# Recurrent chunks of the third and fourth batch at every second slot instead of every third, in a fused mLSTM, Fourier and MLP kernel

## The chip, the cores and the metric

The kernel runs on one core of one Trainium2 chip. Its time is the device time of one execution in microseconds; 439.55 us is the median of three runs of the kernel before (439.53 to 440.16). Five engines each work through an instruction list of their own and wait for one another by semaphores: PE multiplies matrices, DVE (VectorE), ACT (ScalarE) and POOL (GpSimd) do elementwise work, and SP issues the DMAs.

## What is computed

Two blocks, one after the other, on four batches of 768 tokens. The first is a recurrence over time for eight heads of 40 features; its output is the input `x` (768 x 320) of the second. The second adds to `x` the real part of a two-dimensional Fourier transform, normalizes, and adds a two-layer MLP (320 to 1280 to 320):

```python
for t in range(S):                                   # _attn_ref
    m_new = np.maximum(f_gate[:, :, t] + m, i_gate[:, :, t])
    f_stab = np.exp(f_gate[:, :, t] + m - m_new)
    i_stab = np.exp(i_gate[:, :, t] - m_new)
    C = f_stab * C + i_stab * outer(vt, kt)
    n = f_stab * n + i_stab * kt
    denom = np.maximum(np.abs(n @ qt), 1.0)
    y[:, :, t] = sigmoid(o_gate[:, :, t]) * (C @ qt) / denom
...
X = np.fft.fft(np.fft.fft(x, axis=1), axis=2)        # _moe_ref
u = x + np.real(X)
un = (u - mu) / np.sqrt(var + 1e-06)
out = u + np.maximum(un @ w_ch1, 0.0) @ w_ch2
```

## The kernel before

**Tiling.** Each batch is cut into six chunks of 128 tokens (`NT = 6`). Batches are numbered 0 to 3 here, so the change concerns batches 2 and 3. For each chunk the recurrence becomes a handful of matrix products: scores of queries and keys (`mlstm_scores`, L456, into two PSUM tiles `ps`), the contribution of the state carried in (`mlstm_from_state`, L470, into `ph`), that of the chunk itself (`mlstm_from_chunk`, L477, into the same `ph`), and the update of the state (`mlstm_to_state`, L487, into `pc`). Around them: ACT takes exponentials of a decay matrix `W` (`mlstm_exp`, L412, four heads at a time), POOL masks it (`mlstm_mask`, L434), scales the queries (L422) and the values (L428) and decays the state (L446), DVE multiplies the scores into `W` (`mlstm_weigh`, L462), `mlstm_gather` adds `pc` to the state on DVE (L504, L506) and copies `ph` to `hT` on ACT (L508 to L519), `mlstm_turn` transposes `hT` on PE into `px` (L526), and `mlstm_finish` divides and gates on DVE (L535 to L541) and leaves a slice of `x`.

**The Fourier mix** of a batch follows its six chunks: `mix_fold` (DVE, L595 to L607) adds and subtracts pairs of chunks, three folds a batch; then products `pz`, `pzt` (L635 to L638) and `pu` (L669), `mix_add` (DVE, L684 to L694, six a batch), `mix_center` (ACT, L702), transposes `put` (L709) and copies `uT` (ACT, L714).

**The MLP** of batches 1 to 3 has two stages. In the first, five blocks of four steps (`mlp_block`, L829 and L834) form the first layer from sums of its inputs; its four PSUM banks are freed by ACT copies and by DVE additions (L838), and POOL applies the ReLU (L841). In the second, twelve half products per batch (`mlp_out`, L882) form the second layer in PSUM tile `po`, and after every second one `mlp_store` (DVE, L888) writes a tile of the output. `mlp_sums` (DVE, L817) prepares the sums of the first stage just before it begins.

**Order.** The program is laid out by hand. A call `at(slot, phase, fn, ...)` puts work into a numbered slot, and `run` emits slots in order, within a slot by phase (`EVAC` 0, `FILL` 1, `MAIN` 2, `FILL_PE` 3) and at equal phase in the order of the `at` calls, which go batch by batch. Every engine executes its own instructions in the order in which they were emitted. `MAIN` holds one MLP step or half product per slot. The MLP of batch 1 takes slots 63 to 82 for its first stage and 83 to 94 for its second; batch 2 takes 95 to 114 and 115 to 126. Slots 51 to 62 hold the second products of batch 0.

Chunk `c` of a batch starts at slot `s = s0 + stride * c`: exponentials at `s` and `s + 1`, scores at `s`, mask at `s + 1`, `mlstm_weigh` and the state's decay at `s + 2`, the products with state and chunk and the state's update at `s + 3`, `mlstm_gather` at `s + 4`, transposes at `s + 5` to `s + 8`, and `mlstm_finish` a slot later. With stride 3, batch 2 (from slot 50) and batch 3 (from slot 82) have their last two chunks partly beside the first stage of another batch's MLP.

**Buffers.** `ps` has two PSUM banks, so the scores of one chunk wait until the chunk before it has been weighed; `ph`, `pc` and `px` share two banks; the MLP and the mix share four. In SBUF the queries and keys and `W` have three buffers each, `Gb` and `qg` two each, keys and values four.

Of the kernel before, what the change touches and what calls it, by code (L numbers as in the profile page):

```python
# [20 lines left out]
NT = S // L  # L21
# [29 lines left out]
def kernel(  # L51
# [61 lines left out]
    def at(slot, phase, fn, *args):  # L113
        plan.setdefault((slot, phase), []).append((fn, args))
# [7 lines left out]
    EVAC, FILL, MAIN, FILL_PE = range(4)  # L122
# [421 lines left out]
    def plan_mlstm(b, s0, stride=3):  # L544
        for c in range(NT):
            s = s0 + stride * c
            if b > 0:
                t = 22 + 2 * c if b == 1 and c < 3 else s - 5
                at(t, FILL, mlstm_load, b, c)
                at(t, FILL, mlstm_load_max, b, c)  # L550
                at(t, FILL, mlstm_load_decay, b, c)
                at(s, FILL, mlstm_load_o, b, c)
            if (b, c) > (0, 0):
                at(s, FILL, mlstm_exp, b, c, 0)
                at(s + 1, FILL - 0.5, mlstm_exp, b, c, NP)
                last = (b, c) == (0, NT - 1)
                at(s - 1 if last else s, FILL_PE + (2.05 if last else 2), mlstm_scores, b, c)
                if b > 0:
                    at(s + 1, FILL, mlstm_mask, b, c)
            at(s, FILL, mlstm_scale_v, b, c)  # L560
            at(s if (b, c) == (0, 2) else s + 1, FILL + 0.1, mlstm_scale_q, b, c)
            at(s + 2, FILL, mlstm_decay, b, c)
            end = (b, c) == (0, NT - 1)
            at(s + 1 if end else s + 2, FILL - 0.4 if end else FILL, mlstm_weigh, b, c)
            at(s + 2 if end else s + 3, FILL_PE, mlstm_from_state, b, c)
            at(s + 2 if end else s + 3, FILL_PE + (2 if end else 3), mlstm_from_chunk, b, c)
            at(s + 3, FILL_PE + 3, mlstm_to_state, b, c)
            at(s + 3 if end else s + 4, FILL, mlstm_gather, b, c)
            if b == 0:
                t, x = ((8, 11), (11, 14), (13, 14), (14, 15.5), (17, 18), (18, 21))[c]  # L570
            else:
                t = s + (8, 8, 7, 5, 5, 5)[c]
                x = t + 1
            at(t, FILL_PE + ((2.5 if c < 4 else 1) if b == 0 else 1), mlstm_turn, b, c, b == 0 and c < 4)
            at(x, FILL + 0.05, mlstm_finish, b, c)
# [157 lines left out]
    def plan_mix(b, s0, x_done, s_feat, s_add, s_turn):  # L733
        for j in range(TG):
            p = TG - 1 - j
            at(x_done[j], FILL + 0.5, mix_fold, b, p)
            if b == 0:
                at((s0 - 4, s0 - 2, s0)[j], FILL_PE + 4, mix_seq, b, p, (0, 1))
                at((s0 - 2, s0 - 2, s0)[j], FILL_PE + 4, mix_tail, b, p)
            else:  # L740
                at(s0, FILL_PE + 4, mix_seq, b, p, (0,))
                at(s0 + 1, FILL_PE + 4, mix_seq, b, p, (1,))
                at(s0 + 2, FILL_PE + 4, mix_tail, b, p)
        for i in range(2):
            at(s0 + 1 if b == 0 else s0 + 1 + i, FILL, mix_seq_out, b, i)
        at(s0 + (1 if b == 0 else 3), FILL + 0.1, mix_tail_out, b)
        for p in range(TG):
            at(s_feat[p], FILL_PE + 4, mix_feat, b, p)
        for c, a, t in zip(ORDER, s_add, s_turn):
            at(a, FILL, mix_add, b, c)  # L750
            at(t, FILL + 0.1, mix_center, b, c)
            at(t, FILL_PE + 5, mix_turn, b, c)
            if b > 0:
                at(t, FILL_PE + 6, mix_turn_out, b, c)
            elif t < s_mlp:
                at(t + 1, FILL + 0.2, mix_turn_out, b, c)
            else:
                at(t + 1, EVAC, mix_turn_out, b, c)
# [133 lines left out]
    MLP_SLOTS = NT // TG * (NFF + 2 * TG)  # L892

    def plan_mlp(b, s):
        groups = range(NT // TG)
        for i in range(NFF // 2) if b > 0 else ():
            for step in range(4):
                at(s, MAIN, mlp_block, b, i, step)
                s += 1
        for gr in groups if b == 0 else ():  # L900
            for f in range(NFF):
                at(s, MAIN, mlp_in, b, gr, f)
                s += 1
                if f % 2:
                    at(s, EVAC, mlp_relu, b, gr, f - 1)
                    at(s, EVAC, mlp_relu, b, gr, f)
        for gr in groups:
            for i in range(TG):
                for half in range(2):
                    at(s, MAIN, mlp_out, b, gr, i, half)  # L910
                    s += 1
                at(s, EVAC, mlp_store, b, gr, i)
# [3 lines left out]
    gates(gates_pool.enter_context(tc.tile_pool(name="gates", bufs=1)))  # L916


    def plan_batch(b, s_mlstm, s_mix, s_mlp):
        plan_mlstm(b, s_mlstm)  # L920
        done = [s_mlstm + 3 * (j + NT // 2) + 7 for j in range(NT // 2)]
        assert s_mix >= done[-1] and s_mlp >= s_mix + 9
        late = [s_mlp + 2 * c for c in range(TG)]
        if b == 0:
            feat = [s_mix + 1, s_mix + 1, s_mlp + 3]
            turn = [s_mix + 2, s_mix + 3, s_mix + 4]
            add = turn + [s_mlp, s_mlp + 4, s_mlp + 6]
            late = [s_mlp + 2, s_mlp + 5, s_mlp + 7]
        else:
            feat = [s_mix + 3, s_mix + 4, s_mix + 6]  # L930
            add = [s_mix + c for c in (4, 4, 5, 6, 7, 7)]
            turn = [s_mix + c for c in (5, 6, 6)]
            late = [s_mix + c for c in (7, 8, 8)]
            at(s_mlp - 1, FILL_PE + 7, mlp_sums)
        plan_mix(b, s_mix, done, feat, add, turn + late)
        at(s_mlp + NFF, FILL + 0.6, mix_rstd, b)
        plan_mlp(b, s_mlp)

    s_mlp = 31
    plan_batch(0, 0, 22, s_mlp)  # L940
    plan_batch(1, 32, 54, s_mlp + MLP_SLOTS)
    plan_batch(2, 50, 83, s_mlp + 2 * MLP_SLOTS)
    plan_batch(3, 82, 115, s_mlp + 3 * MLP_SLOTS)
    for n in range(4):
        at(s_mlp + 2 * NFF + 1 + n, FILL + 0.4, weight_sums, n)

# [130 lines left out]
```

## Time and profile before

| quantity | value |
|---|---|
| median of three runs | 439.55 us |
| the profiled execution | 440.03 us |
| its span, first to last instruction | 438.3 us |
| granted TensorE clock | 1.00 |
| second products of batch 0, slots 51 to 62 | 123.3 to 181.8 us |
| first stage of batch 1's MLP, slots 63 to 82 | 181.8 to 225.9 us |
| scores of batch 3's chunk 0 at the end of slot 82, then second products of batch 1, slots 83 to 94 | 225.9 to 285.0 us |
| first stage of batch 2's MLP, slots 95 to 114 | 285.0 to 325.9 us |

What a slot is worth differs: the ten matmul instructions of one half product of the second layer take 2.69 us by the chain of waits, one block of four slots of the first stage 6.4 us (205.70 to 212.1 us in the timeline of PE). The profile prints a matmul with its end modelled, so neighbouring rows overlap by some tenths; the distance from one start to the next is the better measure. About 1.7 us of the profiled execution lie outside its span.

### The profile page before, as it was taken

Reading aid. Unit: us, or ns where it says so; the run is one execution under the profiler, and the core shown is the slowest. Engines: PE = TensorE matmul, PEld = TensorE weight load, DVE = VectorE, ACT = ScalarE, POOL = GpSimd, SP = SyncE. Lnnn points to the kernel's source line nnn. Section 1 sums busy time; section 2 is a strip of 40 time slices with the busy share of each in tenths; the row PEclk is TensorE's granted clock in tenths of the full one; section 3 lists DMA queues with packets and bytes.
Section 4 is the critical chain, followed back from the end, with each engine's and each line's share of the span. In section 5 each row is a group of like instructions: output and inputs, shape, how many; then the busy total and the mean of one; then the engine's idle time right before and its main releaser. Section 6 shows DMA issues by size and latency. Waiting matters only on the chain.

```text
span 438.3 us, 7352 instructions
## 1 busy us (share of the span) xinstructions
PE 423.6 (97%) x2696; PEld 285.8 (65%) x2696; DVE 249.7 (57%) x617; ACT 169.6 (39%) x448; POOL 161.3 (37%) x180
## 2 busy tenths in 40 slices
PE   8998999999999999979999999999999999999997
PEld 6877555666577777656456778766456766445774
DVE  7799877589977176587622546677631552343111
ACT  6986376667544204543242334353220131232000
POOL 5554211365424303256581330536670000577000
PEclk9999999999999999999999999999999999999999
DMA  7799396669545424086003334200000000000000
GB/s 237 249 251 336 94 272 226 204 197 271 148 124 163 133 82 133 0 238 184 0 0 92 102 124 137 80 31 3 0 0 16 15 30 31 0 0 2 30 30 30
DMA packets 20547, 47.11 MB, mean 107 GB/s; under 512 B 2784, under 2 KB 9312, under 8 KB 20384
## 3 DMA queue, kind: packets, MB, share of 16 engines
q1 hardware_dynamic: 20512, 46.65, 34.8%
q8 instruction: 21, 0.34, 0.4%
q14 instruction: 14, 0.11, 0.1%
HBM read 42.52 MB, written 4.11 MB: 106 GB/s over the span
## 4 chain that ended last, share of the span: by engine, by line
PE 78%; DVE 12%; issue 4%; DMA 2%; ACT 2%; POOL 1%; SPq 0%; ACTq 0%; POOLq 0%; DVEq 0%
PE po L882 30%; PE pm L829 13%; PE ps L456 5%; PE ph L477 5%; PE ph L470 4%; PE pu L669 4%; PE pm L834 3%; PE pz L638 3%; PE pm L770 3%; PE px L526 2%; PE put L709 2%; PE pzt L638 2%; DMA raw<-in_w 1%; DVE W L462 1%; PE pc L487 1%
## 5 line engine op out<-in xcount | busy, mean ns | idle before, releaser
L882 PE MATMUL po<-w_sb,hT 128*128 128x320 f32 x480 | 135.2, 434 | 0.0
L882 PEld LDWEIGHTS po<-w_sb,hT 128*128 128x128 f32 x480 | 89.7, 190 | 38.1 <-issue 2.0
L841 POOL TENSOR_SCALAR hT<-hT 128x384 f32<-128x384 f32 x45 | 66.4, 1500 | 76.1 <-DVE hT L838 75.8
L888 DVE SCALAR_TENSOR_TENSOR ot<-po,rstd,u 128x320 f32<-128x320 f32 x24 | 13.2, 548 | 69.9 <-PE po L882 69.9
L838 DVE TENSOR_TENSOR hT<-hT,pm 128x384 f32<-128x384 f32 x60 | 30.5, 550 | 39.2 <-ACT hT L859 25.7
L434 POOL TENSOR_SCALAR_AFFINE_SELECT W<-W 128x1024 f32<-128x1024 f32 x18 | 21.0, 1169 | 86.3 <-ACT W L412 65.0
L412 ACT ACTIVATE W<-W,colT 128x128 f32<-128x128 f32 x144 | 45.1, 396 | 0.0
L829 PE MATMUL pm<-uT,w_sb 128*128 128x384 f32 x90 | 32.8, 493 | 2.5 <-DVE hT L838 2.4
L462 DVE TENSOR_TENSOR W<-ps,W 128x512 f32<-128x512 f32 x48 | 30.6, 679 | 6.9 <-POOL W L434 6.7
L770 PE MATMUL pm<-uT,w_sb 128*128 128x384 f32 x80 | 29.8, 500 | 0.5 <-DVE u L691 0.4
L714 ACT COPY uT<-put 128x384 f32<-128x384 f32 x24 | 10.9, 479 | 48.0 <-PE put L709 48.0
L456 PE MATMUL ps<-qk 40*128 40x128 f32 x384 | 28.1, 284 | 0.0
L456 PEld LDWEIGHTS ps<-qk 40*128 40x128 f32 x384 | 23.7, 187 | 4.5 <-issue 1.0
L477 PE MATMUL ph<-W,kvt 128*41 128x128 f32 x384 | 25.8, 277 | 0.0
L422 POOL TENSOR_TENSOR qg<-qk,Gb 128x512 f32<-128x512 f32 x18 | 25.5, 1414 | 0.1
L470 PEld LDWEIGHTS ph<-qg,C 128*128 128x128 f32 x160 | 20.2, 191 | 7.8 <-issue 4.2
L829 PEld LDWEIGHTS pm<-uT,w_sb 128*128 128x128 f32 x90 | 16.0, 190 | 14.0 <-DVE hT L838 6.4
L470 PE MATMUL ph<-qg,C 128*128 128x128 f32 x160 | 21.7, 279 | 2.6 <-DVE x L541 1.0
L834 PE MATMUL pm<-uT,w1t_sb 64*128 64x384 f32 x120 | 23.9, 509 | 0.0
L477 PEld LDWEIGHTS ph<-W,kvt 128*41 128x41 f32 x384 | 19.5, 117 | 3.0 <-DVE fe L602 0.2
L515 ACT COPY h<-ph 41x512 f32<-41x512 f32 (+1 forms) x16 | 9.3, 580 | 28.8 <-PE ph L477 28.7
L702 ACT ACTIVATE uc<-u 128x384 f32<-128x384 f32 x24 | 14.1, 612 | 15.0 <-DVE u L694 15.0
(166 smaller groups left out, 641.3 us busy)
## 6 DMA issues: line engine op xcount, KB each, us to landing
W<-M_d SPq DMA_DIRECT2D x18, 512.0 KB
kvt<-in_kv SPq DMA_DIRECT2D x24, 324.0 KB
qk<-in_qkT SPq DMA_DIRECT2D x48, 160.0 KB
raw<-in_w SPq DMA_DIRECT2D x10, 640.0 KB
Gb<-G_d SPq DMA_DIRECT2D x36, 128.0 KB
so<-in_o SPq DMA_DIRECT2D x24, 160.0 KB
out<-ot SPq DMA_DIRECT2D x24, 160.0 KB
ds_sb<-in_dft_s SPq DMA_DIRECT2D x1, 1155.0 KB
```

The lines of the kernel that those rows point to most:

```text
L412: nc.scalar.activation(out=k.W[:, h, :], in_=M, func=AF.Exp, scale=-1.0, bias=colT[:, c, 0, b * H + h:b * H + h + 1])
L422: nc.gpsimd.tensor_tensor(out=k.qg, in0=k.qk[:, 0], in1=k.Gb, op=OP.mult)
L456: nc.tensor.matmul(k.ps[hip][:, p, :], k.qk[r, 1, p, :], k.qk[r, 0, p, :], start=True, stop=True)
L462: nc.vector.tensor_tensor(out=Wv, in0=k.ps[hip], in1=Wv, op=OP.mult)
L470: nc.tensor.matmul(k.ph[:, p, :], k.C[:, p, :], k.qg[:, p, :], start=(p == 0), stop=False, skip_group_check=True)
L477: nc.tensor.matmul(k.ph[hip * 64:hip * 64 + D1, p, :], k.v1[:, 2 * p + hip, :], k.W[:, 2 * p + hip, :], start=(c == 0 and p == 0), stop=Tr ...
L770: nc.tensor.matmul(k.pm[i], w1_sb[:, ch, f0:f0 + L], u[2 * ch], start=(ch == 0), stop=False)
L829: nc.tensor.matmul(bank, w, u, start=start, stop=True, skip_group_check=True)
L834: nc.tensor.matmul(bank, block(w1t_sb, i)[rows], mlp_u(gr, 1)[rows], start=False, stop=True, skip_group_check=True)
L838: nc.vector.tensor_tensor(out=h, in0=h, in1=bank, op=OP.add)
L841: nc.gpsimd.tensor_scalar(out=h, in0=h, scalar1=-1.0, scalar2=0.0, op0=OP.mult, op1=OP.max)
L882: nc.tensor.matmul(k.po, k.h[gr][f][:, i * L:(i + 1) * L], w2_sb[:, f, :], start=(f == 0), stop=(f == NFF - 1))
```

## The change

The chunks of batches 2 and 3 come every second slot instead of every third, and start one slot later (51 and 83 instead of 50 and 82), so that all scores lie beside the second products of the batch before. Loads are issued later relative to the chunk, each kind at a slot of its own, and `mlstm_turn` is at `s + 6` for chunks 0 to 4 and `s + 5` for chunk 5. The folds follow the finished pairs of chunks, so they move too: for batch 2 from slots 66, 69 and 72 to 64, 66 and 68, for batch 3 from 98, 101 and 104 to 96, 98 and 100. Batches 0 and 1 and all of the mix and the MLP stay in their slots.

```diff
@@ plan_mlstm
             s = s0 + stride * c
             if b > 0:
-                t = 22 + 2 * c if b == 1 and c < 3 else s - 5
-                at(t, FILL, mlstm_load, b, c)
-                at(t, FILL, mlstm_load_max, b, c)
-                at(t, FILL, mlstm_load_decay, b, c)
-                at(s, FILL, mlstm_load_o, b, c)
+                t = [22 + 2 * c] * 3 if b == 1 and c < 3 else [s - 5] * 3 if stride > 2 else (s - 4, s - 2, s - 3)
+                at(t[0], FILL, mlstm_load, b, c)
+                at(t[1], FILL, mlstm_load_max, b, c)
+                at(t[2], FILL + 0.2, mlstm_load_decay, b, c)
+                at(s, FILL + 0.3, mlstm_load_o, b, c)
...
-                t = s + (8, 8, 7, 5, 5, 5)[c]
+                t = s + ((8, 8, 7, 5, 5, 5) if stride > 2 else (6, 6, 6, 6, 6, 5))[c]
                 x = t + 1
@@ plan_batch
-    def plan_batch(b, s_mlstm, s_mix, s_mlp):
-        plan_mlstm(b, s_mlstm)
-        done = [s_mlstm + 3 * (j + NT // 2) + 7 for j in range(NT // 2)]
+    def plan_batch(b, s_mlstm, s_mix, s_mlp, stride=3):
+        plan_mlstm(b, s_mlstm, stride)
+        done = [s_mlstm + stride * (j + NT // 2) + 7 for j in range(NT // 2)]
...
-    plan_batch(2, 50, 83, s_mlp + 2 * MLP_SLOTS)
-    plan_batch(3, 82, 115, s_mlp + 3 * MLP_SLOTS)
+    plan_batch(2, 51, 83, s_mlp + 2 * MLP_SLOTS, 2)
+    plan_batch(3, 83, 115, s_mlp + 3 * MLP_SLOTS, 2)
```

## The prediction, made before the changed kernel ran

> **What bounds the kernel now.** I read the page's busy times first, then the busy times of four stretches (the stages in which the moved work lies), then who waited for whom in them, and last the timelines of PE and DVE. The page says that PE is the bound:
>
> ```profile
> span 438.3 us, 7352 instructions
> PE 423.6 (97%) x2696; PEld 285.8 (65%) x2696; DVE 249.7 (57%) x617; ACT 169.6 (39%) x448; POOL 161.3 (37%) x180
> ```
>
> The four stretches, in order: second products of batch 0, first stage of batch 1, second products of batch 1 (with the scores of batch 3's chunk 0 ahead of them), first stage of batch 2.
>
> ```profile
> core 0: us, PE busy (x) PEld busy (x) DVE busy (x) ACT busy (x) POOL busy (x), PEclk, DMA share, GB/s
> 123.30:181.80 58.50, 58.50 (x416) 44.11 (x417) 32.14 (x84) 18.82 (x53) 14.47 (x19) 1.00 0.37 114
> 181.80:225.90 44.10, 40.33 (x210) 22.91 (x208) 30.74 (x81) 17.35 (x45) 26.97 (x23) 1.00 0.37 105
> 225.90:285.00 59.10, 59.10 (x429) 44.63 (x429) 26.64 (x74) 21.41 (x61) 20.10 (x24) 1.00 0.31 99
> 285.00:325.90 40.90, 39.72 (x209) 23.50 (x208) 26.61 (x76) 14.30 (x35) 23.07 (x20) 1.00 0.03 9
> ```
>
> Beside the second products PE is never idle. Beside the first stages it is idle for 44.10 - 40.33 = 3.8 and 40.90 - 39.72 = 1.2 us. The change moves PE work from the second and fourth stretch into the first and third and takes none away, so at most these 5.0 us can be won. Who PE waits for in 184.9 to 226.9 us:
>
> ```profile
> PE pm L829 <- DVE hT L838: 1.2, 2, 0.8
> PE ph L470 <- DVE x L541: 1.0, 1, 1.0
> PE px L526 <- DVE C L506: 0.6, 1, 0.6
> ```
>
> All of it is DVE coming late, which at this point is working off a queue (timeline of DVE): `mlp_sums` from 182.57, then a store, the gather, the weighing, two finishes, an addition, and a fold.
>
> ```profile
> 185.59 0.54 DVE L888 SCALAR_TENSOR_TENSOR ot<-po,rstd,u 128x320 f32<-128x320 f32 x1
> 186.05 0.67 DVE L506 TENSOR_TENSOR C<-C,pc 40x164 f32<-40x164 f32 x2
> 186.75 1.29 DVE L462 TENSOR_TENSOR W<-ps,W 128x512 f32<-128x512 f32 x2
> 189.11 0.49 DVE L541 TENSOR_TENSOR x<-px,so 128x320 f32<-128x320 f32 x1
> 189.52 0.54 DVE L838 TENSOR_TENSOR hT<-hT,pm 128x384 f32<-128x384 f32 x1
> 194.11 0.49 DVE L595 TENSOR_TENSOR eo<-x 128x320 f32<-128x320 f32 x1
> 195.46 0.32 DVE L602 TENSOR_TENSOR fe<-eo 128x159 f32<-128x159 f32 x1
> ```
>
> From starts to starts: sums 0.59 each, store 0.46, gather 0.70, weighing 1.21, finish 1.56 (187.96 to 189.52), fold 1.71 (194.11 to 195.82), addition 0.47.
>
> [...] the weighing at 174.71 (below) starts only when two whole `mix_add` are done. [...] `so<-so,den` (L539) took 1.36 us at 190.61, while POOL masked and scaled queries, and 0.49 at 188.58.
>
> **The change part by part.** PE prices, from starts in the timeline: scores of a chunk 1.09, from state 0.98, from chunk 1.00, state update 0.41, transposes 0.44.
>
> *Moved PE work.* Into each of the two stages of second products come two sets of scores, one chunk's three products and one set of transposes: 2.18 + 2.39 + 0.44 = +5.0. Out of each first stage go one set of scores, the same three products and one set of transposes: -3.9. The other set of scores leaves slot 50 or slot 82: -1.09. Sum zero.
>
> *Weighing just ahead of the next scores.* This decides. With stride 3, the scores of chunk c+1 came one slot after the weighing of chunk c, whose `ps` banks they need. With stride 2 both are in the same slot: PE reaches the scores after one half product (2.69), and by then DVE must have done all that it has in this slot ahead of the weighing. Where batch b's `mix_add`s are in the slot, they are emitted first (lower batch number), and they wait for `pu`, the last PE product of the slot before. The trace shows such a run of DVE work:
>
> ```profile
> 170.47 0.44 PE L669 MATMUL pu<-dd_sb,Zt 128*1 128x161 f32 x2
> 171.55 2.86 PE L882 MATMUL po<-w_sb,hT 128*128 128x320 f32 x10
> ...
> 170.95 0.33 DVE L684 TENSOR_TENSOR u<-x,pu 128x161 f32<-128x161 f32 x1 [1.17 <-PE pu L669]
> 174.61 0.18 DVE L694 BATCH_NORM_AGGREGATE u<-stats 128x2 f32<-128x6 f32 x1
> 174.71 1.26 DVE L462 TENSOR_TENSOR W<-ps,W 128x512 f32<-128x512 f32 x2
> ```
>
> Two `mix_add` take 3.3 us (155.86 to 159.17), with the row of their own as here 3.8. Slot by slot, from its first PE instruction:
> - slot 87 (batch 3): two adds 3.3, gather 0.7, weighing 1.3 = 5.3; PE is there at 2.7. Stall 2.6.
> - slot 61 (batch 2): adds begin 0.8 early (six transposes `put` stand between) and end at 3.0, gather 3.7, weighing 5.0; PE, with transposes of chunk 2 on the way, is there at 3.1. Stall 1.8.
> - slot 59: one add 1.7, gather and weighing to 3.7, PE at 3.1. Stall 0.6. Slot 89: its add needs no new `pu`, DVE is done at 1.7. None. Slots 53, 55, 57, 85, 91, 93 have no add ahead of the weighing (the two of slot 90 are over by then): DVE is done 0.5 to 2.5 after the slot's start. None.
> - slot 58: the state update of chunk 2 has been given the PSUM bank of its own `ph`, so it waits for the copies of `ph` on ACT (0.58 + 0.17 and two handovers). Stall 0.8. Slot 90: it waits for the finish of chunk 0 behind two adds, which ends as PE arrives. 0.1.
>
> Sum: 3.2 in the first stage of second products, 2.7 in the other. What queues behind the waiting scores on PE is everything: the rest of the slot and all later ones, and PE has no spare time to make it up.
>
> *First stages.* DVE loses a weighing, a gather and a finish here, but the folds come closer together and two of them ahead of the additions that free PE's banks. Batch 1's stage, from slot 63 at 0: DVE begins with the sums at 0.8 (as before: 182.57), is done with them at 3.1, store 3.6, gather 4.3, weighing 5.5, finish 7.1, fold 8.8, addition 9.2, finish 10.8, fold 12.5, three additions 13.9, finish 15.5, fold 17.2, addition 17.7. PE: transposes of chunk 3 until 2.0; from state waits for the gather (4.3 against 3.4); from chunk waits for the weighing (5.5 against 5.3); the tails of block 0 wait for the addition (9.2 against 8.5); block 1 waits for the next additions (13.0 against 11.6) and its own tails again (17.7 against 17.2). PE finishes block 1 at 19.6, and three more blocks of 6.4 with the 0.36 of idling that PE has at 212.83 behind the norm factors (L722 to L731) make 39.1; 0.2 for joints: 39.3 against 44.1. Batch 2's stage: `mlp_sums` are out of the way before it starts (its mix is three slots earlier), DVE runs ahead until the second fold: finish 3.6, fold 5.2, addition 5.7, finish 8.4, fold 10.1, additions from 10.5 (PE there at 9.4), last fold 14.7, addition 15.1 (PE 14.6). It ends at 36.9 against 40.9.
>
> So the first stages get shorter by 4.8 and 4.0, of which 3.9 each is the moved work: 1.0 us of idling is won, not 5.0, because the same DVE queue stands there with its folds pushed together.
>
> *Loads, masks, exponentials.* ACT needs about 2.6 for eight exponentials (8 x 0.32 by starts, 182.42 and 186.59) and some 1.2 for copies and the gate per chunk, POOL 1.17 + 1.41 + 0.82 + 2 x 0.50 = 4.4; a chunk now has two slots of 9 to 12 us. Both fit, and masks end a slot or more before the weighing. The loads of `W` are freed by the products at `s - 3` and asked for at `s - 2`: two slots for 512 KB, hidden unless a transfer takes over some 9 us. Their SP instructions stand behind an output store that waits for DVE, which in these slots is done early. I take 0; if the cover is gone, ACT, mask, weighing and scores slip, up to 3.
>
> *Joints.* Scores stand alone now; the half product after lone scores at 226.91 took 0.1 longer. Twelve places: 0 to 1.2, and as much may be saved where scores leave other products. I take 0.
>
> **Sum,** against the profiled execution: second products +5.0 + 3.2 and +5.0 + 2.7; slots 50 and 82 -1.1 each; first stages -4.8 and -4.0. Together +4.9, so 440.03 becomes 444.9. The median shown is 0.48 below that execution: 444.5.
>
> **Rivals.**
> 1. *Waits as reckoned* (chance 0.60): 444.5, its own range 442.0 to 447.5 (stalls of 59, 58 and 87 half or one and a half times their size, joints).
> 2. *The folds' move frees the first stages* (0.10, faster). One mechanism: additions that free PE's banks stop being late there, all 5.0 us of idling go, and the stalls in the second products come out under 3 us: 439.55 - 5.0 + 2.5 = 437. For it: DVE has 3.6 us less to do per first stage. Against: fold and finish stand ahead of the additions in the emitted order, as now. It decides in favour of faster as soon as the new stalls are below the idling that is won.
> 3. *An even trade* (0.08): stalls of 5.9 shrink to 1 or the idling won grows to match: 439.5.
> 4. *More than reckoned* (0.22): POOL, now busier beside the second products, holds up DVE's finishes and folds (0.9 each, as at 190.61; about four on the path), or loads of `W` land late (3): 444.5 + 4 = 448.5.
>
> **How the numbers follow.** About 0.2% is what a measurement here can tell from no change. Slower: rivals 1 and 4 and a little of 3, 0.84; within 0.2%: 0.06; faster 0.10. The range 439.5 to 449.5 leaves about 0.13 below and 0.06 above.
>
> **What would show it.** In the changed profile the scores (L456) of slots 61 and 87 wait for DVE's W (L462), 1.8 and 2.6 us; PE is idle some 6 us in the two stages of second products, where it is never idle now; the first stages last about 39 and 37 us with 1 to 1.4 us waits for hT (L838) at block 1. I am wrong if L456 has no waits, or if the first stages lose more than 6 us each.

## The result and the profile after

| | before | after |
|---|---|---|
| median | 439.56 us (439.19 to 440.94, 6 runs) | 452.82 us (451.84 to 455.75, 6 runs) |
| the profiled execution | 440.03 us | 452.77 us |
| its span | 438.3 us | 451.1 us |
| granted TensorE clock, mean of an execution | 1.00 in the profiled one | 0.989 to 0.996 in all six |

The ratio is 1.0304 with an interval of 1.0273 to 1.0335. The change makes the kernel 13.3 us slower: the direction forecast, more than twice the size (444.5), and above the range (up to 449.5).

The page of the kernel after, against the same lines of before:

```profile
span 451.1 us, 7344 instructions
PE 433.7 (96%) x2696; PEld 288.2 (64%) x2696; DVE 245.5 (54%) x617; ACT 169.0 (37%) x448; POOL 159.5 (35%) x180
PEclk9999999999999999999999979999999999999999
```

PE executes the same 2696 products and is busy 10.1 us longer with them (433.7 against 423.6). At an equal count the rows themselves have become longer. Part of that is waiting inside a row, which the profile counts as busy: the scores of slot 59 take 1.75 us (at 167.64) and no idling is shown ahead of them, where 1.16 is usual. Part is the clock: the one 7 in its row (slices of 11.3 us) shows where it fell.

The busy times of the four stages of after, each from the first product of the stage to the first of the next. The columns are the stretch, its length, the busy time of PE, PEld, DVE, ACT and POOL with counts, the granted clock, and the DMA share and rate:

```profile
core 0: us, PE busy (x) PEld busy (x) DVE busy (x) ACT busy (x) POOL busy (x), PEclk, DMA share, GB/s
121.37:189.68 68.31, 66.03 (x494) 49.11 (x493) 33.52 (x95) 25.36 (x75) 19.71 (x25) 1.00 0.32 96
189.68:229.53 39.85, 38.38 (x149) 19.80 (x148) 25.65 (x72) 11.69 (x27) 19.76 (x16) 1.00 0.37 98
229.53:300.58 71.05, 68.19 (x489) 50.62 (x487) 30.67 (x83) 25.73 (x75) 24.54 (x29) 0.95 0.32 93
300.58:338.45 37.87, 37.00 (x151) 19.65 (x148) 23.13 (x67) 10.97 (x25) 19.76 (x16) 1.00 0.01 4
```

I call them A (second products of batch 0), B (first stage of batch 1), C (second products of batch 1) and D (first stage of batch 2), and cut every kernel in this way. In the kernel before, the scores in slot 82 then belong to B.

| | start of A | A | B | C | D | D's end to the end of the span |
|---|---|---|---|---|---|---|
| before | 123.22 | 58.58 | 45.11 | 58.04 | 40.77 | 112.6 |
| after | 121.37 | 68.31 | 39.85 | 71.05 | 37.87 | 112.6 |
| difference | -1.85 | +9.73 | -5.26 | +13.01 | -2.90 | 0 |

A and C grow by 22.7 us, of which 10.0 is the work that moved into them; the rest of that growth, 12.7, is about as much as the whole profiled execution lost. Who PE waited for, over the whole span of after (engine, what, line, releaser: sum, times, longest):

```profile
PE ps L456 <- issue: 2.1, 1, 2.1
PE ps L456 <- DVE W L462: 1.3, 1, 1.3
...
PE pm L834 <- DVE hT L838: 0.9, 2, 0.5
...
PE pc L487 <- ACT h L519: 0.8, 1, 0.8
...
PE pc L487 <- DVE x L541: 0.6, 1, 0.6
```

The scores (L456) now wait twice as idling of PE, in slots 87 and 61, and the state's update (L487) in slots 58 and 90. The place of the longest of them, slot 87, in the timeline of PE of after (start, duration, what, and the idle time ahead of it):

```profile
251.45 2.85 PE L882 MATMUL po<-w_sb,hT 128*128 128x320 f32 x10
256.44 2.47 PE L456 MATMUL ps<-qk 40*128 40x128 f32 x16 [2.14 <-issue]
258.84 1.43 PE L669 MATMUL pu<-dd_sb,Z 128*128 128x161 f32 x4
260.07 1.27 PE L669 MATMUL pu<-dd_sb,Zt 128*128 128x320 f32 x2
261.13 4.30 PE L882 MATMUL po<-w_sb,hT 128*128 128x320 f32 x10
```

and DVE over the same time, of which the first row is the start of two `mix_add`, the second and third the end of them and the gather, the last the weighing:

```profile
251.65 0.33 DVE L684 TENSOR_TENSOR u<-x,pu 128x161 f32<-128x161 f32 x1 [2.04 <-PE pu L669]
...
254.87 0.18 DVE L694 BATCH_NORM_AGGREGATE u<-stats 128x2 f32<-128x6 f32 x1
254.97 0.65 DVE L504 COPY C<-pc 40x164 f32<-40x164 f32 x2
255.65 1.29 DVE L462 TENSOR_TENSOR W<-ps,W 128x512 f32<-128x512 f32 x2
```

Two additions take 3.32 us (251.65 to 254.97), gather and weighing 1.97; the scores start at 256.44, when the second of the weighing's two instructions is under way. DVE ran them in the order of emission: it stood idle for 2.04 us ahead of the first addition, waiting for `pu`, although the scores that this weighing takes had started at 242.87 (1.16 us) and the mask on POOL at 238.54 (1.09 us). The trace names "issue" for this wait, where it names DVE's `W` in slot 61: the releaser is inferred, and here the instruction that ends the wait is read from DVE's timeline. The wait is the one that the prediction gave for slot 87.

What it did not give is in the last row of PE. Ten products of a half take 4.14 us from their start to the next (261.13 to 265.27; 2.69 before), and the six products of `pu` 2.29 from their start to that of the half product (258.84 to 261.13), where those of slot 86 took 1.19 (250.26 to 251.45). The clock over this stretch of after, cut where it changes (columns as above, the clock third from the end):

```profile
253.81:257.22 3.41, 1.13 (x6) 0.51 (x6) 3.00 (x9) 0.82 (x3) 1.67 (x4) 1.00 0.74 223
257.22:260.64 3.42, 3.42 (x20) 3.00 (x20) 0.00 (x0) 0.00 (x0) 2.27 (x2) 0.50 0.00 0
260.64:264.05 3.41, 3.41 (x8) 2.23 (x7) 1.69 (x6) 0.00 (x0) 0.00 (x0) 0.50 0.23 82
264.05:267.46 3.41, 3.41 (x45) 2.90 (x44) 1.95 (x6) 0.00 (x0) 0.00 (x0) 1.00 0.14 48
```

The granted clock is down to 0.50 for 6.83 us, from 257.22, 0.8 us after the scores began, to 264.05. A wait of 2.1 us has a second price here, paid after it is over.

### The profile page after: what moved, and what is told of

Read it like the earlier page. It is cut to its first block, busy times and chain, and to the rows that moved or that the text cites. A ratio compares the mean times of both kernels' runs of the same rounds, so it can differ in the third digit from the quotient of the medians.

```text
span 451.1 us, 7344 instructions
## 1 busy us (share of the span) xinstructions
PE 433.7 (96%) x2696; PEld 288.2 (64%) x2696; DVE 245.5 (54%) x617; ACT 169.0 (37%) x448; POOL 159.5 (35%) x180
## 4 chain that ended last, share of the span: by engine, by line
PE 73%; DVE 15%; DMA 5%; issue 4%; POOL 1%; ACT 1%; DVEq 0%; ACTq 0%; POOLq 0%; SPq 0%
PE po L882 28%; PE pm L829 12%; PE ps L456 5%; PE ph L477 4%; PE pu L669 4%; PE pm L834 3%; PE ph L470 3%; PE pz L638 3%; DMA kvt<-in_kv 2%; DVE W L462 2%; DVE hT L838 2%; PE px L526 2%; DMA qk<-in_qkT 2%; PE pzt L638 2%; DMA raw<-in_w 1%
## 5 line engine op out<-in xcount | busy, mean ns | idle before, releaser
L882 PE MATMUL po<-w_sb,hT 128*128 128x320 f32 x480 | 137.2, 438 | 0.0
L882 PEld LDWEIGHTS po<-w_sb,hT 128*128 128x128 f32 x480 | 90.7, 192 | 39.0 <-issue 3.4
L456 PE MATMUL ps<-qk 40*128 40x128 f32 x384 | 30.2, 290 | 3.8 <-issue 2.1
L456 PEld LDWEIGHTS ps<-qk 40*128 40x128 f32 x384 | 25.2, 191 | 10.1 <-issue 5.8
L834 PE MATMUL pm<-uT,w1t_sb 64*128 64x384 f32 x120 | 26.1, 512 | 0.9 <-DVE hT L838 0.9
L446 POOL TENSOR_TENSOR C<-C,decB 40x164 f32<-40x164 f32 x24 | 11.6, 484 | 41.6 <-DVE C L506 36.9
L829 PEld LDWEIGHTS pm<-uT,w_sb 128*128 128x128 f32 x90 | 16.2, 190 | 13.5 <-DVE hT L838 4.3
L834 PEld LDWEIGHTS pm<-uT,w1t_sb 64*128 64x128 f32 x120 | 12.3, 185 | 12.9 <-issue 7.4
```

The lines of the kernel that those rows point to most:

```text
L456: nc.tensor.matmul(k.ps[hip][:, p, :], k.qk[r, 1, p, :], k.qk[r, 0, p, :], start=True, stop=True)
L829: nc.tensor.matmul(bank, w, u, start=start, stop=True, skip_group_check=True)
L834: nc.tensor.matmul(bank, block(w1t_sb, i)[rows], mlp_u(gr, 1)[rows], start=False, stop=True, skip_group_check=True)
L882: nc.tensor.matmul(k.po, k.h[gr][f][:, i * L:(i + 1) * L], w2_sb[:, f, :], start=(f == 0), stop=(f == NFF - 1))
```

## The experiments

The theory that these runs test, as it stands at their end: the +13 is the score waits as forecast, a halved clock that follows them, and a price for scores that stand alone between other products; and the first stages win no idling since DVE's queue stands as before. Rivals: most of the loss comes from the moved products being dearer (contention on DVE, POOL or DMA), or the first stages are the cause. Every median below is set against runs of the kernel before on the same chip in the same session.

**1. The additions behind the weighing.** In stages A and C `mix_add` is emitted after the weighing of its slot, in place of ahead of it; nothing else moves.

```diff
@@ after
-            at(a, FILL, mix_add, b, c)
+            at(a, FILL + (0.04 if b in (1, 2) else 0), mix_add, b, c)
```

> The changed kernel, with mix_add of batches 1 and 2 emitted behind the gather and the weighing of the same slot. Theory 1 (the scores wait for a weighing that stands behind mix_add in DVE's queue; the longest of these waits also lowers the clock): the waits of L456 for W (L462) go, 2.6 us in slots 59 and 61 and 2.9 in slot 87, and with them some 3.5 us of lowered clock; clock 1.00, about 444 us. Theory 2 (the weighing itself is late, because loads of W, exponentials or masks are): order changes nothing, 451 to 453 us.

445.30 us; 1.0110 (1.0079 to 1.0141). The scores wait nowhere, the clock is 0.999 or 1.00 in all four executions, A is 65.69 and C 64.98. In A that is 2.62 less than in after, all of it the waits of slots 59 and 61 (scores to next half product: 2.1 and 2.1 in after, 1.5 and 1.5 here, and half product to scores in slot 61 4.6 against 3.2). This one edit takes away more than half of the loss.

**2. The idling of slot 87 filled.** Five products that nobody reads keep PE busy while the scores of slot 87 wait; the wait itself stays.

```diff
@@ after
+    at(87, FILL_PE + 1.9, idle_products, 5, ps_m, "pm")
```

> The changed kernel with five products that nobody reads, some 2.2 us of PE work, ahead of the scores of slot 87, where PE otherwise stands still. Theory A (PE's standing still lowers its clock): the granted clock stays 1.00, the products after the scores take their usual time (pu 1.2 and po 2.7 instead of 2.3 and 4.1 us), about 449.3 us. Theory B (the clock falls there for another reason, such as the work done until then): the clock stays near 0.992 and the time near 452.8 us.

451.05 us; 1.0248 (1.0206 to 1.0290), which as a median is not told from after. The four executions fall apart by clock: 449.79 and 449.87 at 1.00, 452.22 at 0.996 and 453.51 at 0.992. The profiled one is at 1.00, and there the half product after the scores is back at its old length; timeline of PE of this kernel:

```profile
256.82 1.75 PE L456 MATMUL ps<-qk 40*128 40x128 f32 x16
...
259.69 2.85 PE L882 MATMUL po<-w_sb,hT 128*128 128x320 f32 x10
262.38 1.05 PE L470 MATMUL ph<-qg,C 128*128 128x128 f32 x8
```

C is 67.74, against 71.05 in after: 3.31 are the clock, and 67.74 - 64.98 = 2.76, against experiment 1, are the wait. The filling doesn't cure the clock in every execution. The 1.3 us of idling in slot 61 are still there and may be what halves it in the other two; experiment 3 has this gap alone, and one of its four executions is at 0.996. That is weak evidence, since the kernel before, without such a gap, was at 0.996 in one of 23 executions beside experiment 9, and no trace shows it.

**3. and 4. Each batch alone.** Only batch 2, and only batch 3, gets stride 2.

```diff
@@ after (3)
-    plan_batch(3, 83, 115, s_mlp + 3 * MLP_SLOTS, 2)
+    plan_batch(3, 82, 115, s_mlp + 3 * MLP_SLOTS)
@@ after (4)
-    plan_batch(2, 51, 83, s_mlp + 2 * MLP_SLOTS, 2)
+    plan_batch(2, 50, 83, s_mlp + 2 * MLP_SLOTS)
```

> Stride 2 for batch 2 alone; batch 3 as in the kernel before. Theory 1: its waits are those of slots 58 to 61, too short to lower the clock: clock 1.00, about 443 us. Theory 2 (loads and masks late, in both stages alike): about 446 us.

> Stride 2 for batch 3 alone; batch 2 as in the kernel before. Theory 1: the wait in slot 87 and the lowered clock are both here: clock about 0.992, about 448.5 us. Theory 2: about 446 us, as batch 2 alone.

444.87 us, 1.0112 (1.0080 to 1.0143), and 447.22 us, 1.0168 (1.0138 to 1.0197). The stages add up: with batch 2 alone A is 68.31 as in after and C and D are as before (58.04 and 40.77), its executions at 1.00 take 444.42 to 445.03 and the one at 0.996 takes 447.20; with batch 3 alone A is as before (58.58) and D as in after (37.86). C is 67.76 there and not 71.05, although the scores wait just as long. Timeline of PE of the kernel with batch 3 alone:

```profile
252.82 1.72 PE L456 MATMUL ps<-qk 40*128 40x128 f32 x16 [2.14 <-issue]
...
255.66 2.58 PE L882 MATMUL po<-w_sb,hT 128*128 128x320 f32 x9
```

and its busy times, with the clock (third from the end), just after the gap:

```profile
255.00:258.00 3.00, 3.00 (x14) 2.20 (x13) 1.69 (x6) 0.00 (x0) 0.88 (x1) 1.00 0.14 49
```

The same 2.14 us of idling, and the clock stays at 1.00: whether such a gap halves the clock differs by execution. This one took 445.87 us, the three others 447.16 to 449.02 with clocks of 0.992 to 0.996. So waits and clock are two terms, and only the first is there each time. Experiments 2 and 4 give the same C (67.74 and 67.76) by different ways, which settles the size of the second: 3.3 in the profiled execution of after. The busy times of PE agree: 427.4 and 426.7 us in the two profiles here, both at full clock, are together 6.9 over before, which leaves 3.2 of the 10.1.

**5. Scores one slot later.** In the stride-2 batches the scores go to the chunk's second slot, so that the weighing of the chunk before is a slot ahead of them again. They then share their slot with the products of the chunk before.

```diff
@@ after
-                at(s - 1 if last else s, FILL_PE + (2.05 if last else 2), mlstm_scores, b, c)
+                at(s - 1 if last else s if stride > 2 else s + 1, FILL_PE + (2.05 if last else 2), mlstm_scores, b, c)
```

> The changed kernel with the scores of batches 2 and 3 a slot later, beside the products of the chunk before, so that the weighing ahead of them has a slot more and the scores no longer stand alone on PE. Theory 1 (what is left of the loss after the waits is the joints at lone scores, some 0.1 us each way, and two waits of the state's update): no waits of L456, clock 1.00, about 443 us, below the kernel with mix_add behind the weighing. Rival (the joints cost nothing; the rest lies elsewhere): as that kernel, about 445 us.

442.63 us; 1.0061 (1.0039 to 1.0082), clock 1.00 throughout. A is 64.06 and C 63.88, that is +5.48 and +5.84 over before, of which 5.01 is moved work. So no more than 0.5 and 0.8 of these stages are anything else: all but a little of what after has over the moved work goes with where the scores stand. This is against the rival of dearer products: they are the same products, with the same loads and masks beside them. B and D stay at 39.83 and 37.86.

**6. and 7. The folds.** The theory on the first stages says that DVE's folds stand ahead of the additions that free PE's banks. Here the folds of batches 2 and 3 go four slots apart, up to the start of the mix: in the kernel before, and in kernel 5.

```diff
@@ plan_batch
+        if b > 1:
+            done = [s_mix - 12, s_mix - 8, s_mix - 4]
```

> The kernel before, with only the folds of batches 2 and 3 put later, to the first slot of the third, fourth and fifth block of the first stage. Theory 1 (PE waits there for additions behind the folds): the waits of L829 for hT go, the two first stages are 1 to 1.5 us shorter each, about 437.5 us. Rival (finishes and sums are what makes the additions late): no change.

> The changed kernel with the scores a slot later and the folds of batches 2 and 3 late. Theory 1: first stages of about 38 and 36.5 us instead of 39.85 and 37.87, so some 3 us less than with the scores alone, about 440 us. Rival (the first stages are bound by finishes and the gather): as with the scores alone.

In the kernel before: 438.15 us, 0.9956 (0.9943 to 0.9969); B loses 1.06, D 1.08. In kernel 5: 438.19 us, 0.9957 (0.9947 to 0.9967); B loses 2.42 (37.41), D 1.85 (36.01). So the folds' places are worth about twice as much with stride 2 as with stride 3 (4.27 against 2.14 in B and D together). The two kernels take the same time: once the folds are late, stride 2 with later scores is no faster than stride 3. DVE's timeline in B, first of after (finish, fold, addition; second fold and three additions), where the stage begins at 189.68:

```profile
196.22 0.49 DVE L541 TENSOR_TENSOR x<-px,so 128x320 f32<-128x320 f32 x1
196.75 0.49 DVE L595 TENSOR_TENSOR eo<-x 128x320 f32<-128x320 f32 x1
...
198.34 0.55 DVE L838 TENSOR_TENSOR hT<-hT,pm 128x384 f32<-128x384 f32 x1
...
202.16 1.48 DVE L838 TENSOR_TENSOR hT<-hT,pm 128x384 f32<-128x384 f32 x3
```

then of kernel 7, where it begins at 186.78:

```profile
193.32 0.49 DVE L541 TENSOR_TENSOR x<-px,so 128x320 f32<-128x320 f32 x1
193.73 0.54 DVE L838 TENSOR_TENSOR hT<-hT,pm 128x384 f32<-128x384 f32 x1
195.33 0.17 DVE L535 TENSOR_SCALAR den<-px 128x8 f32<-128x8 f32 x1 [1.06 <-PE px L526]
...
196.91 1.47 DVE L838 TENSOR_TENSOR hT<-hT,pm 128x384 f32<-128x384 f32 x3
```

From the start of the stage, the first addition comes at 8.66 in after and at 6.95 with the folds out of the way, the three additions at 12.48 and 10.13; and DVE now waits for PE (the 1.06 ahead of the finish) and not the other way round.

**8. Lone scores.** To measure a joint by itself: in the kernel before, with stride 3, the scores of chunks 0 to 3 of batches 2 and 3 move from the slot of the products to a slot of their own, a slot later. Nothing waits for them there, and no work is added.

```diff
@@ before
-                at(s - 1 if last else s, FILL_PE + (2.05 if last else 2), mlstm_scores, b, c)
+                at(s - 1 if last else s + 1 if b > 1 and c < 4 else s, FILL_PE + (2.05 if last else 2), mlstm_scores, b, c)
```

> The kernel before, with the scores of chunks 0 to 3 of batches 2 and 3 a slot later, where they stand alone between products of the MLP or the mix; nothing waits longer for it. If a joint costs what the remainder of the changed kernel asks for (about 0.1 to 0.15 us each), the two stages of second products get some 0.5 us longer each, and the kernel 1 us slower. If joints cost nothing, no change.

441.65 us; 1.0036 (1.0023 to 1.0048). A is 60.46: 1.09 of it is the scores of chunk 0 that now lie in it, and 60.46 - 58.58 - 1.09 = 0.79 is new; C has 59.82 - 58.04 - 1.09 = 0.69. Eight lone groups cost 1.5 us, 0.19 each. Timeline of PE of this kernel:

```profile
121.53 2.96 PE L882 MATMUL po<-w_sb,hT 128*128 128x320 f32 x10
124.41 1.16 PE L456 MATMUL ps<-qk 40*128 40x128 f32 x16
125.51 2.96 PE L882 MATMUL po<-w_sb,hT 128*128 128x320 f32 x10
128.30 0.60 PE L526 MATMUL px<-ident,h 128*128 128x128 f32 x4
```

From start to start, a half product ahead of lone scores takes 2.88 and the one after them 2.79, in place of 2.69; the scores take their 1.10. So it is the neighbours that get longer, on both sides. In the kernel before, the half product ahead of these scores took 2.78 (129.15 to 131.93) where they stood beside the products from the chunk, so some 0.1 of the 0.29 here was paid there too; the 0.19 is what standing alone adds.

**9. A gap alone.** Does idling of 2 us halve the clock by itself, without scores, loads or folds? In the last stage of the kernel before, in which DVE has little to do, one product that nobody reads is made to wait for additions on a small tile; 3 of them are over before PE comes, 9 and 12 are not.

```diff
@@ before
+    pad = const.tile([L, 2 * L], FP, name="pad")
...
+    def busy(n):
+        nc.vector.memset(pad, 0.0)
+        for _ in range(n):
+            nc.vector.tensor_tensor(out=pad, in0=pad, in1=pad, op=OP.add)
+
+    def wait_for_pad():
+        pw = ps_s.tile([L, 2 * L], FP, name="pi", tag="ps")
+        nc.tensor.matmul(pw, rest[:, 0:L], pad, start=True, stop=True, skip_group_check=True)
+
+    at(151, FILL, busy, 9)
+    at(151, FILL_PE, wait_for_pad)
```

> The kernel before, with one product that nobody reads in the last second products, and three additions on DVE (and a clearing) that it waits for; they are done before PE is there. Control: clock 1.00, some 0.5 us more than before.

> As the control with nine additions, so that PE waits for DVE about 1 to 1.5 us. If the clock falls only after waits of over 2 us: clock 1.00, 1.5 us more than the control. If any wait can lower it: clock below 0.999 in some executions.

> As the control with twelve additions: PE waits about 2.5 us, as in slot 87 of the changed kernel. If such a wait lowers the clock by itself: about 0.992 in most executions, and 2.5 + 3 us more than the control. If it doesn't: clock 1.00 and 2.5 us more than the control.

| additions | PE idle, profiled | median | ratio to before | clock of the executions |
|---|---|---|---|---|
| 3 | 0 | 440.67 | 1.0011 (0.9998 to 1.0025) | 0.999 or 1.00, one of 20 at 0.996 |
| 9 | 2.36 | 444.57 | 1.0101 (1.0086 to 1.0116) | 0.995 to 0.996, all 4 |
| 12 | 3.74 | 447.80 | 1.0171 (1.0148 to 1.0194) | 0.992 to 0.996, all 4 |

Both gaps came out longer than expected (1 to 1.5 and 2.5), so a gap of 1.3 us, as in slot 61, was not tried alone. From the first to the last product of this stage the profiled executions take 32.89, 37.21 and 38.59 us: 4.32 and 5.70 over the control, and so 1.96 over the gap both times, each with one stretch at half the clock. The medians are 3.9 and 7.1 over the control; two of the four executions with twelve additions have a mean clock of 0.992 and lost more than the profiled one. Timeline of PE with 9 additions:

```profile
418.81 1.22 PE L972 MATMUL pi<-pad,rest 128*128 128x256 f32 x2 [2.36 <-DVE pad L968]
...
419.82 2.71 PE L883 MATMUL po<-w_sb,hT 128*128 128x320 f32 x5
```

and the busy times of the same kernel around it, cut where the clock changes:

```profile
415.41:418.82 3.41, 1.05 (x5) 0.40 (x3) 3.10 (x8) 0.00 (x0) 0.00 (x0) 1.00 0.08 29
418.82:422.24 3.42, 3.42 (x7) 2.45 (x8) 0.00 (x0) 0.00 (x0) 0.00 (x0) 0.50 0.00 0
422.24:425.65 3.41, 3.41 (x14) 2.38 (x14) 0.55 (x1) 0.00 (x0) 0.00 (x0) 1.00 0.09 31
```

The clock is at half for 3.41 us and then back; in after it was twice as long. So here an idle gap of 2.36 us was enough, in 4 of 4 executions, with no other part of the change.

The traces also show in what the gap of slot 87 differed between after, where the clock was halved, and kernel 4, where it was not. The changes of the clock in a trace lie whole multiples of 3.413 us apart: 257.22 and 264.05 in after (2 times), 418.82, 422.24 and 442.72 with nine additions (1 and 6 times). They lie on a grid, then, and it stands differently in the four profiled executions used here: counted from the span's start, its first point is at 1.22 us in after, 2.40 with nine additions, 2.64 with twelve and 3.26 in kernel 4. In after the gap falls into one stretch of it (PE busy 1.13 us), with nine additions too (1.05). In kernel 4, whose clock changes at 443.58 (56 stretches after 252.43), a point of the grid, counted back from there, cuts the gap in two; with twelve additions one cuts it as well, at 419.06, and only the second part is followed by a fall, at 422.48. First kernel 4, then twelve additions:

```profile
249.02:252.43 3.41, 1.66 (x7) 0.83 (x5) 3.21 (x12) 1.99 (x7) 0.58 (x2) 1.00 0.89 239
252.43:255.85 3.42, 2.89 (x23) 2.47 (x24) 0.88 (x2) 0.00 (x0) 3.34 (x4) 1.00 0.13 50
...
415.65:419.06 3.41, 1.79 (x7) 0.95 (x5) 3.17 (x8) 0.00 (x0) 0.00 (x0) 1.00 0.14 48
419.06:422.48 3.42, 1.30 (x5) 1.06 (x6) 1.93 (x5) 0.00 (x0) 0.00 (x0) 1.00 0.00 0
```

In all profiled executions whose grid can be read, apart from their first 10 us and their last stretches, the three stretches in which PE was busy 1.05, 1.13 and 1.30 us are followed by half the clock, and none in which it was busy 1.66 or more. The mean clocks fit: one, two and three stretches at half in 451 us make 0.996, 0.992 and 0.989, the values that after has in its six executions. This is read from three falls after the fact; no run moved a gap against the grid on purpose.

**10. The gather first.** In kernel 7 the products with the state still wait for the gather in stage B, which stands behind `mlp_sums` and a store on DVE. Kernel 10 is kernel 7 with the gather of batch 2's chunk 4 ahead of `mlp_sums` and the weighing of chunk 5 ahead of the store.

```diff
@@ kernel 7
-            at(s + 1 if end else s + 2, FILL - 0.4 if end else FILL, mlstm_weigh, b, c)
+            at(s + 1 if end else s + 2, FILL - 0.4 if end else EVAC - 0.5 if (b, c) == (2, 5) else FILL, mlstm_weigh, b, c)
...
-            at(s + 3 if end else s + 4, FILL, mlstm_gather, b, c)
+            at(s + 3 if end else s + 4, FILL, mlstm_gather, b, c) if (b, c) != (2, 4) else at(s + 3, FILL_PE + 6.9, mlstm_gather, b, c)
```

> The changed kernel with later scores and late folds, and in addition the gather of batch 2's chunk 4 ahead of mlp_sums on DVE and the weighing of chunk 5 ahead of the store. Theory 1 (from state waits for that gather, from chunk for that weighing): the wait of L470 for C (L506) goes, the first stage of batch 1's MLP is about 1 us shorter (36.5 us), the kernel about 437.2 us. Rival (the wait is replaced by one for the sums or an addition a step later): 438 us as before.

The waits of PE from 183 to 226 us, first of kernel 7:

```profile
PE ph L470 <- DVE C L506: 0.7, 1, 0.7
PE pm L829 <- DVE hT L838: 0.4, 1, 0.4
```

then of kernel 10, where the wait for `C` is gone:

```profile
PE pm L829 <- DVE hT L838: 0.4, 1, 0.4
PE pm L829 <- ACT hT L855: 0.2, 1, 0.2
```

437.40 us (436.46 to 437.55, six executions), 0.9920 (0.9904 to 0.9937); B is 36.36, 1.05 less. It is the fastest of all: 3.1 us under the kernel before, 15 under the changed one. Chunks beside the second products do free the first stages: B and D together go from 85.88 before to 72.37 here, and of these 13.5 us 8.9 (4.99 and 3.9) are moved work and 4.6 are waiting that is gone; A and C pay 1.3 over their 10.0 of moved work. But kernel 6 has 2.0 of the 3.1 us with stride 3 and late folds alone, and kernel 7 was no faster than it. The gather first was not tried with stride 3, so no run shows that stride 2 is worth anything by itself. The changed kernel gets none of it, with its scores in the slot of the weighing and its folds ahead of the additions.

## Why the prediction was off

The step that failed is the price of disturbing PE. Where PE would wait, for what and how long was right; but the prediction charged a wait with its length alone and scores that stand alone with nothing. The clock that fell after the gap of 2.14 us cost 3.3 us and the joints 2.35, together 5.65 of the 7.8 us that its sum of 4.9 lacks. The rest is in the first stages, which lost 0.7 us where 1.0 was to be won, and in the state's update (0.8 more).

The sum of the prediction, term by term, beside what the profiled executions and the experiments gave for it (us, after less before):

| term of the sum | predicted | measured | from |
|---|---|---|---|
| moved work, all stages | 0 | 0 | counts: 2696 products in both |
| waits of the scores, slots 59, 61, 87 | 5.0 | 2.62 + 2.76 = 5.4 | A of after less A of 1; C of 2 less C of 1 |
| waits of the state's update, slots 58, 90 | 0.9 | 0.93 + 0.75 = 1.7 | starts in the timeline |
| joints | 0 | 1.17 + 1.18 = 2.35 | what is left of A and C in kernel 1; size by experiment 8 |
| clock | not in the sum | 3.3 | C of after less C of kernel 2, or of kernel 4 |
| idling won in B and D | -1.0 | -0.27 + 1.0 = +0.7 | stages less moved work |
| start of A | 0 | -0.76 | -1.85 less 1.09 of scores |
| sum | +4.9 | +12.7 | profiled: 452.77 - 440.03 |

- *Weighing just ahead of the next scores: right, in place, cause and size.* Slot 87: 2.6 forecast, 2.76 measured. Slots 59 and 61: 2.4 forecast, 2.62 measured. The trace of before had all that was needed: the length of two additions, and the order of emission.
- *The clock: missing from the sum.* The prediction used every price at a clock of 1.00 because before showed nothing else. It named a stall of 2.6 us on an engine that had never been idle there and did not ask what an idle PE does to its clock. The traces show it afterwards: the clock was at 0.50 for 6.83 us in after and for 3.41 us with nine and with twelve additions, its changes lie on the grid of experiment 9, and gaps of 2.14 and 2.36 us were enough when they fell into one stretch of it. How long the half clock lasts differs: one stretch with nine and with twelve additions, two in after.
- *Joints: taken as 0 in a range of 0 to 1.2.* Measured 2.35, with twelve lone groups. This term is what is left over, and experiment 8 gives its size independently: the one instance in before (0.1 behind the lone scores, in the half product at 226.91) was one side of one joint, a group alone costs 0.19 net, and twelve of them 2.3. This is a case where the nearest row was there and its lower half was counted.
- *State's update: half size.* Slot 58 came out at 0.93 for the 0.8 forecast. Slot 90 was 0.75 for 0.1: there the update ends up waiting for the finish (`x`, L541) on DVE, which the prediction had ending just in time. These two waits go in kernel 5, as A and C there show, but no run removed them alone.
- *First stages: the walk on DVE nearly right, block 1 too early.* In B the three additions were forecast from 12.5 after the start and came at 12.48, the last ones from 17.2 and came at 17.46. In D it was 10.5 and 10.50, then 14.7 and 15.48; here the prediction's own prices (1.4, 1.6 and 1.7 for additions, finish and fold) lead from 10.5 to 15.2 and not to the 14.7 that it wrote. PE then needed longer for the tails of block 1, which ended at 20.3 for 19.6 in B and at 18.3 for some 17.1 in D; what follows took the 19.6 forecast in both. So the stages shrank by 4.17 and 2.90 (B without the 1.09 of slot 82's scores), not by 4.8 and 4.0, and the 1.0 of idling that was to be won is 0.7 lost. The cause is the one named, folds pushed together ahead of the additions: moving them gives 2.42 and 1.85 back with stride 2 and 1.06 and 1.08 with stride 3, which leaves 1.36 and 0.77 for the pushing together.
- *Readings that were off without changing the sum.* Not all idling of B in before was DVE's: the waits were read from 184.9 on, and just ahead of that PE waits 0.97 for a copy on ACT (L515, at 183.26). The 1.00 for the products of a chunk is that of a row with no state update behind it (122.22 to 123.22); with one it is 0.90 (133.03 to 133.93). Moved work is then 4.9 in and 3.8 out for 5.0 and 3.9, again with a sum of zero.
- *Loads, masks, exponentials at nothing: held.* PE shows no wait for them in the two stages, and kernel 5 has them all in place with at most 0.5 and 0.8 over the moved work.
- *Rivals.* The likeliest had the mechanisms that are there, without the clock and the joints. The fourth, more than reckoned, had the right direction of the error, but for causes (POOL, loads of `W`) that the runs do not show. The second, folds freeing the first stages, has its mechanism in kernels 6 and 7 and not in the change: it takes folds that move away from the additions, and the change moved them closer.
- *Start of A.* It is 0.76 earlier in after than the moved scores explain. The three kernels of experiment 9 are the kernel before up to there and start A at 123.39, 123.51 and 124.41, so a difference of this size is scatter between executions.

What stays open: why the half clock lasted two stretches in after although PE is busy throughout the first of them, what brings single executions to 0.996 without a gap of 2 us, and how often a gap of some 2 us falls into one stretch (kernel 4: three of four executions below 0.999).

## What to carry to other kernels

A wait that is forecast on PE where it was never idle had two prices here, the gap and what the clock did after it: 2.14 us and then 3.3 in slot 87 of after, 2.36 us and then 1.96 with nine additions, in the profiled executions. Add the second to the range when the forecast gap comes near these lengths. From the half clock alone (0.50 over 3.41 us) it is 1.7 us for each such stretch, an estimate, and by the mean clocks (0.996 to 0.989) the executions of after had one to three of them. When work of an engine that runs it in the order of emission, as DVE did in slot 87, is packed closer, list what every other engine has ahead of its counterpart in that same slot, and consider a shift of the consumer by one slot first: here one slot for the scores was worth some 10 us (kernel 5 against after). And when one engine frees another's buffers, work without a deadline (the folds) goes behind the work that frees, even if it could run sooner: later folds were worth 2.42 and 1.85 us in B and D with stride 2, and 1.06 and 1.08 with stride 3.

## What the hardware showed unexpectedly

An idle gap of PE, 2.36 us in the profiled execution, came with a lowered clock in 4 of 4 executions; in the profiled one the clock was at half for 3.41 us, and the stage took 1.96 us over the gap. The same 2.14 us gap in slot 87 halved the clock in the profiled execution of after and left it at 1.00 in that of kernel 4: the changes of the clock in a trace lie whole multiples of 3.413 us apart, and in these traces it fell after stretches with PE busy 1.30 us or less and not after one with 1.66. Sixteen products over 40 rows between products over 128 rows cost 0.19 us more than beside the other products of the recurrence, and the longer time shows in the neighbours' rows (2.88 and 2.79 for 2.69), not in their own.
